# Splitting the first state load in two, and moving or putting off VectorE work that stood ahead of batch 1's A^T

## The chip, the cores and the metric

One NeuronCore of a Trainium2 chip runs the whole program. The metric is the device time of one execution in microseconds (us), the median over several executions. A profile is one execution: its "span" leaves out some 2 us of start and end that the time includes. Ratios are the mean time of one kernel's fast executions over that of the other's of the same rounds, so not quite the ratio of the medians quoted.

## The reference, cut to what matters

```python
B, H, S, Ns, D = 8, 8, 512, 32, 64
scores = x @ state.T / sqrt(D);  a  = softmax(scores)        # x reads the states
xread  = a @ state
scores2 = state @ x.T / sqrt(D); a2 = softmax(scores2)       # the states read x
sread  = a2 @ x
y = concat([xread, sread]) -> (4352, 512)
out = maximum(y @ w1, y @ w2) @ w_out                        # d_ff = 1024
```

The kernel folds the MoE weights into the states: `wcat` holds W1 - W2 (1024 columns) and W2 @ Wout (512 columns), and per batch `SW = states @ wcat`. Layer 1 of a batch is then `relu(SW^T A^T)`, and layer 2 (l2) adds `r @ Wout` to `A @ SW[:, 1024:]`. So each batch needs x transposed (`xt`) for its scores, the scaled exponents `a`, their transpose `aT`, and SW in three parts of 512 columns.

## The kernel before: the parts that matter

Loads, all on SyncE's (SP's) queue, in this order (s_f are states, xf is x, w2f/w1f/wof the weights):

```python
first, rest = slice(0, 3), slice(3, 8)
load_states(first)                 # 192 KB in rows of 256 B
load_x(0, 2)                       # two halves of 512 KB
for ch in range(2):
    load_w(w2f, moe_w2, ch); load_wo(2 * ch); load_wo(2 * ch + 1)
load_w(w1f, moe_w1, 0); load_w(w1f, moe_w1, 1)     # "W1b" in what follows: the first one, w1f -> w1b
load_x(1); load_states(slice(3, 8)); load_x(2)
```

Every engine runs its list in program order. The stretch that the change reorders (batch 0's second half beside batch 1's scores):

```python
compact_x(1, 0); compact_x(1, 1)   # ACT: two casts of x to bf16, 1.0 us each
d_xt(1)                            # transpose by DMA
...
u_sw(0, 1); l2_add(0, 3, ...); l1(0, {}, range(4, 8))
u_exp(1, 0); u_exp(1, 1)           # TensorE scores, ACT exp
u_norm(1, 0, nc.vector)            # DVE: sum, reciprocal, scaling a <- e, er
u_norm(1, 1, nc.gpsimd)            # the scaling on GpSimd
cast_x(2)
l2_add(0, 0, range(4, 8)); l2_close(0, 0)          # l2_close: copy PSUM -> SBUF, DVE for even, ACT for odd
u_sw(1, 0)                                         # SW part 0 of batch 1: matmuls, a copy on DVE, one on ACT
u_sr(1)
l2_add(0, 1, range(4, 8)); l2_close(0, 1)
u_sw(1, 1)
compact_x(2, 0); compact_x(2, 1); d_xt(2)          # ACT, then DMA
l2_add(0, 2, range(4, 8)); l2_close(0, 2)
u_sw(1, 2); u_at(1, "V")                           # A^T: TensorE transposes, copy on DVE
l2_add(0, 3, ...); u_srt(1); l2_close(0, 3); l2_out(0)
for b in range(1, B): l1(b, fill) ...              # regular from here
```

The softmax here doesn't subtract the row's maximum and nothing guards it: scores larger than these inputs give would overflow.

Of the kernel before, what the change touches and what calls it, by code (L numbers as in the profile page):

```python
# [15 lines left out]
def kernel(  # L16
# [14 lines left out]
    nc = tc.nc  # L31
# [5 lines left out]
    NC = S // 128  # L37
# [15 lines left out]
    def bank(dtype=F32, kind="ps"):  # L53
        return pools[kind].tile([128, 512 if dtype == F32 else 1024], dtype, tag="b", name=kind)
# [4 lines left out]
    def copy(eng, o, i):  # L59
        if eng == "A":  # L60
            nc.scalar.copy(o, i)  # L61
        elif eng == "V":
            nc.vector.tensor_copy(o, i)  # L63
        else:
            nc.gpsimd.tensor_copy(o, i)  # L65
# [4 lines left out]
    def run(*units):  # L70
        for u in units:
            u()
# [4 lines left out]
    def load_x(b, parts=1):  # L77
        xf_t[b] = xio.tile([128, H, NC * D], F32, tag="xf", name="xf")
        for g in range(parts):
            nc.sync.dma_start(out=xf_t[b][:, g::parts, :], in_=x[b, g::parts].rearrange("h (p c) d -> p h (c d)", c=NC))  # L80
# [3 lines left out]
    def load_states(bs):  # L84
        nc.sync.dma_start(out=s_f[:, 2 * bs.start:2 * bs.stop],
                          in_=state[bs].rearrange("b (q h) n d -> (h n) (b q) d", q=2))

    first, rest = slice(0, 3), slice(3, 8)
    w2f = stage.tile([128, 4, FF], F32)
    w1f = stage.tile([128, 4, FF], F32)  # L90
    wof = stage.tile([128, NF, DM], F32)
# [1 line left out]
    def load_w(t, w, ch):  # L93
        cs = slice(ch * 512, (ch + 1) * 512)
        nc.sync.dma_start(out=t[:, :, cs], in_=w.rearrange("(i p) f -> p i f", p=128)[:, :, cs])
# [10 lines left out]
        load_wo(2 * ch + 1)  # L106
    load_w(w1f, moe_w1, 0)
    load_w(w1f, moe_w1, 1)
    load_x(1)
    load_states(slice(3, 8))  # L110
    load_x(2)

    ident = consts.tile([128, 128], BF16)
# [20 lines left out]
    def cast_states(eng, bs):  # L134
        qs = slice(2 * bs.start, 2 * bs.stop)
        copy(eng, s_bf[:, qs], s_f[:, qs].unsqueeze(2).to_broadcast([128, qs.stop - qs.start, 2, D]))
# [12 lines left out]
    def states(bs):  # L149
        p = bank(BF16)  # L150
        n = bs.stop - bs.start
        for q in range(2 * n):
            nc.tensor.transpose(p[:, q * 128:(q + 1) * 128], s_bf[:, 2 * bs.start + q].rearrange("p u d -> p (u d)"), ident)
        for g in range(2):
            copy("V", sbd[64 * g:64 * g + 64, bs, :, g, :],
                 p[64 * g:64 * g + 64, 0:256 * n].rearrange("p (b h n) -> p b h n", b=n, h=H))
# [16 lines left out]
    def cast_x(b, parts=(("P", slice(0, 8)),)):  # L173
        new_x(b)
        xp = st[b]["xp"] = xio.tile([128, H, NC, 66], BF16, tag="xp", name="xp")
        nc.gpsimd.memset(xp[:, :, :, 64:65], 1.0)
        for e, hs in parts:
            copy(e, xp[:, hs, :, 0:64], xf_t[b][:, hs].rearrange("p h (c d) -> p h c d", c=NC))

    def compact_x(b, g, eng="A"):  # L180
        new_x(b)
        if g == 0:
            st[b]["xc"] = at.tile([128, H, NC * D], BF16, tag="xc", bufs=1, name="xc")
        copy(eng, st[b]["xc"][:, 4 * g:4 * g + 4], xf_t[b][:, 4 * g:4 * g + 4])


    def d_xt(b):
        nc.sync.dma_start_transpose(out=st[b]["xt"], in_=st[b]["xc"].rearrange("p h w -> p (h w)"))
# [14 lines left out]
    def u_exp(b, g):  # L203
        d = st[b]
        if g == 0:
            d["e"] = at.tile([128, 2, 4, NC, Ns], BF16, tag="e", name="e")
            d["es"] = at.tile([128, 2, 4 * NC], F32, tag="es", name="es")
            d["er"] = at.tile([128, 2, 4 * NC], F32, tag="er", name="er")
            d["a"] = at.tile([128, 2, NC, 4, Ns], BF16, tag="a", name="a")
        p = bank()  # L210
        for i in range(4):
            for cp in range(2):
                k = 2 * i + cp
                nc.tensor.matmul(p[:, k * 64:k * 64 + 64],  # L214
                                 d["xt"][:, 4 * i + 2 * g + cp, :], sbd[:, b, 2 * i + g].rearrange("p u n -> p (u n)"),
                                 start=(k == 0), stop=(k == 7))
        nc.scalar.activation(out=d["e"][:, g].rearrange("p i c n -> p (i c n)"), in_=p, func=ACTF.Exp, scale=scale)  # L217

    def u_norm(b, g, mul):
        d = st[b]  # L220
        nc.vector.tensor_reduce(d["es"][:, g], d["e"][:, g].rearrange("p i c n -> p (i c) n"),  # L221
                                axis=mybir.AxisListType.X, op=ALU.add)
        nc.vector.reciprocal(d["er"][:, g], d["es"][:, g])
        mul.tensor_mul(  # L224
            d["a"][:, g].rearrange("p c i n -> p i c n"), d["e"][:, g],
            d["er"][:, g].rearrange("p (i c) -> p i c", i=4).unsqueeze(3).to_broadcast([128, 4, NC, Ns]))
# [41 lines left out]
    def sw_mm(b, ch, engs="VA"):  # L268

        pg = [bank(kind="acc" if ch == 2 and b > 1 else "ps") for g in range(2)]  # L270

        two = (b, ch) == (0, 0)
        terms = ((sbd, w1b), (sneg, w2b)) if two else ((sbd, wcat),)
        for k, (sv, w) in enumerate(terms):
            for i in range(4):
                for g in range(2):
                    gs = slice(64 * g, 64 * g + 64)
                    nc.tensor.matmul(pg[g][32 * i:32 * i + 32, :],  # L278
                                     sneg[gs, i, :] if k else sbd[gs, b, 2 * i + g, g, :],
                                     w[gs, i, ch * 512:(ch + 1) * 512],  # L280
                                     start=(k == 0), stop=(k == len(terms) - 1))
        return lambda: [copy(engs[g], SW[b][:, g, ch * 512:(ch + 1) * 512], pg[g]) for g in range(2)]

    def u_sw(b, *chs):
        for out_of in [sw_mm(b, ch) for ch in chs]:
            out_of()
# [4 lines left out]
    def relu(o, p, eng=None):  # L291
        flip[0] ^= 1
        if eng == "A" or (eng is None and flip[0]):
            nc.scalar.activation(out=o, in_=p, func=ACTF.Relu)  # L294
        else:
            nc.vector.tensor_scalar(o, p, scalar1=0.0, scalar2=None, op0=ALU.max)  # L296
# [3 lines left out]
    def l1(b, fill, fs=range(NF), engs=None):  # L300
        if fs[0] == 0:
            R[b] = big.tile([128, NF, NC * 128], BF16, tag="r", name="r")
        for f in fs:
            p = bank()
            for g in range(2):
                nc.tensor.matmul(p, SW[b][:, g, f * 128:(f + 1) * 128], AT[b][:, g, :], start=(g == 0), stop=(g == 1))  # L306
            relu(R[b][:, f, :], p, engs and engs[f - fs[0]])
            run(*fill.get(f, ()))
# [3 lines left out]
    def l2_open(b, c):  # L312
        if c == 0:
            OB[b] = [big.tile([128, NC, DM], F32, tag="ob", name="ob")] + [None] * NC
        OB[b][1 + c] = acc()
        for g in range(2):
            nc.tensor.matmul(OB[b][1 + c], AT[b][:, g, c * 128:(c + 1) * 128], SW[b][:, g, FF:WC], start=(g == 0), stop=False)  # L317

    def l2_add(b, c, fs):
        for f in fs:  # L320
            nc.tensor.matmul(OB[b][1 + c], R[b][:, f, c * 128:(c + 1) * 128], wo[:, f, :], start=False, stop=(f == NF - 1))  # L321

    def l2_close(b, c):
        ob = OB[b][0]
        dst = out[b * L:b * L + S].rearrange("(p c) n -> p c n", c=NC)
        copy("A" if c % 2 else "V", ob[:, c, :], OB[b][1 + c])
        if b == B - 1:
            nc.sync.dma_start(out=dst[:, c:c + 1], in_=ob[:, c:c + 1])

    def l2_out(b):  # L330
        nc.sync.dma_start(out=out[b * L:b * L + S].rearrange("(p c) n -> p c n", c=NC), in_=OB[b][0])
# [156 lines left out]
    compact_x(1, 0)  # L488
    compact_x(1, 1)
    d_xt(1)  # L490
    cast_states("P", rest)
    cast_x(1)
    load_x(3)
    sT = d_states(rest)
    for c in range(NC):
        l2_open(0, c)
    for c in range(NC - 1):
        l2_add(0, c, range(0, 4))
    u_sw(0, 1)
    l2_add(0, 3, range(0, 4))  # L500
    l1(0, {}, range(4, 8))
    u_exp(1, 0)
    u_exp(1, 1)
    u_norm(1, 0, nc.vector)
    u_norm(1, 1, nc.gpsimd)
    cast_x(2)
    l2_add(0, 0, range(4, 8))
    l2_close(0, 0)
    u_sw(1, 0)
    u_sr(1)  # L510
    l2_add(0, 1, range(4, 8))
    l2_close(0, 1)
    u_sw(1, 1)
    compact_x(2, 0)
    compact_x(2, 1)
    d_xt(2)
    l2_add(0, 2, range(4, 8))
    l2_close(0, 2)
    u_sw(1, 2)
    u_at(1, "V")  # L520
    l2_add(0, 3, range(4, 6))
    u_srt(1)
    l2_add(0, 3, range(6, 8))
    l2_close(0, 3)
    l2_out(0)
    for b in range(1, B):
        fill = fillers(b)
# [40 lines left out]
```

## Time and profile before

| | us |
|---|---|
| time, median of 6 executions | 151.78 (151.63 to 151.95) |
| span of the profiled execution | 149.5 (that execution: 151.25, faster than any unprofiled one) |
| TensorE busy | 139.9, 94% of the span |
| VectorE (DVE), ScalarE (ACT), GpSimd (POOL) busy | 82.3, 75.0, 42.8 |

The prediction shows the lines of the chain of waits and of TensorE's waits. To read the chain: each line is the piece of work that the end waited for at that time, so an engine named there is what the kernel stood on; what is not named there can be busy without costing anything.

### The profile page before, as it was taken

What the parts mean: (1) busy time and instruction counts of PE and PEld (TensorE: products, weight loads), DVE (VectorE), ACT (ScalarE), POOL (GpSimd) and SP (SyncE); (2) the same over time, 40 slices, a digit from 0 to 9 for tenths busy, and PEclk for the clock granted to TensorE, in tenths of its full rate; (3) what the DMA queues carried; (4) which work ended last, traced back from release to release, by engine and by line L of the source; (5) the groups of instructions that cost most, each with busy time, mean ns of one, the idle gap of its engine ahead of it and who ended that gap; (6) DMA issues with size and microseconds to landing.
All of it is one profiled execution on the core that took longest, in us unless ns stands there. A gap on an engine that the chain in (4) does not pass through costs nothing.

```text
span 149.5 us, 2991 instructions
## 1 busy us (share of the span) xinstructions
PE 139.9 (94%) x1229; PEld 67.7 (45%) x1249; DVE 82.3 (55%) x149; ACT 75.0 (50%) x126; POOL 42.8 (29%) x45
## 2 busy tenths in 40 slices
PE   6988999999799999999999999999999999999990
PEld 1454633424345445434543454344445434764460
DVE  5538528947968097726754582658067625721120
ACT  3157447545958157626844682478167036521010
POOL 3145359670934510550073017104100500000000
PEclk9999999999999999999999999999999999999999
DMA  4999999988599958983979397850556031502423
GB/s 112 381 387 387 388 385 326 293 157 262 113 246 295 266 110 259 305 154 87 289 253 203 117 304 206 154 246 35 111 104 281 2 75 44 237 0 70 142 96 120
DMA packets 37950, 29.89 MB, mean 200 GB/s; under 512 B 24880, under 2 KB 33328, under 8 KB 37040
## 3 DMA queue, kind: packets, MB, share of 16 engines
q1 hardware_dynamic: 37792, 29.56, 68.0%
q8 instruction: 10, 0.16, 0.4%
q10 hardware_dynamic: 144, 0.13, 0.3%
q14 instruction: 4, 0.03, 0.1%
HBM read 15.20 MB, written 8.91 MB: 161 GB/s over the span
## 4 chain that ended last, share of the span: by engine, by line
PE 73%; DMA 13%; DVE 6%; SPq 4%; issue 2%; ACT 1%
PE acc L321 32%; PE ps L306 18%; DMA w1f<-in_moe_w_dram 10%; PE acc L317 9%; DMA xt<-xc 3%; PE ps L365 2%; PE acc L375 2%; PE ps L278 2%; PE ps L214 2%; SPq L98 2%; DVE swt L63 2%; PE acc L355 1%; PE ps L237 1%; PE acc L373 1%; DVE es L221 1%
## 5 line engine op out<-in xcount | busy, mean ns | idle before, releaser
L321 PE MATMUL acc<-wo,r 128*128 128x512 bf16 x239 | 58.3, 379 | 0.6 <-issue 0.2
L321 PEld LDWEIGHTS <-r 128*128 128x128 bf16 x248 | 23.9, 98 | 28.5 <-issue 0.5
L296 DVE TENSOR_SCALAR r<-ps 128x512 bf16<-128x512 f32 x32 | 22.1, 691 | 14.7 <-PE ps L306 14.7
L306 PE MATMUL ps<-aT,swt 128*128 128x512 bf16 x127 | 29.1, 379 | 1.2 <-DVE aT L63 0.9
L224 POOL TENSOR_TENSOR a<-e,er 128x512 bf16<-128x512 bf16 x13 | 13.4, 1049 | 57.3 <-ACT e L217 27.2
L63 DVE COPY ob<-acc 128x512 f32<-128x512 f32 (+1 forms) x17 | 11.1, 652 | 30.2 <-PE acc L321 29.8
L61 ACT COPY ob<-acc 128x512 f32<-128x512 f32 (+1 forms) x16 | 9.1, 572 | 28.6 <-PE acc L321 21.0
L294 ACT ACTIVATE r<-ps 128x512 bf16<-128x512 f32 x32 | 19.2, 601 | 7.0 <-PE ps L306 6.4
L306 PEld LDWEIGHTS <-swt 128*128 128x128 bf16 x128 | 12.1, 98 | 15.8 <-issue 1.1
L317 PE MATMUL acc<-swt,aT 128*128 128x512 bf16 x56 | 16.7, 380 | 1.0 <-issue 1.0
L61 ACT CAST swt<-ps 128x512 bf16<-128x512 f32 x18 | 9.9, 588 | 14.0 <-PE ps L278 14.0
L65 POOL CAST xp<-xf 128x2048 bf16<-128x2048 f32 (+1 forms) x8 | 14.1, 1761 | 9.1 <-DMA xf<-in_x_dram 9.1
L61 ACT CAST xc<-xf 128x1024 bf16<-128x1024 f32 x14 | 14.0, 1052 | 1.1 <-DMA xf<-in_x_dram 1.1
L221 DVE TENSOR_REDUCE es<-e 128x16 f32<-128x512 bf16 x16 | 10.6, 662 | 4.0 <-ACT e L217 4.0
L63 DVE CAST swt<-ps 128x512 bf16<-128x512 f32 x18 | 11.7, 680 | 1.2 <-PE ps L278 1.2
L217 ACT ACTIVATE e<-ps 128x512 bf16<-128x512 f32 x16 | 8.8, 595 | 1.3 <-PE ps L214 0.6
L129 PE MATMUL ps<-warm 128*128 128x512 bf16 x24 | 8.2, 470 | 1.3 <-POOL warm L115 1.3
L410 PE MATMUL acc<-wo,w2t 128*128 128x512 bf16 x30 | 7.3, 379 | 0.1
L317 PEld LDWEIGHTS <-aT 128*128 128x128 bf16 x62 | 4.7, 98 | 6.0 <-issue 2.6
L278 PE MATMUL ps<-wcat,sbd 64*32 64x512 bf16 x136 | 6.3, 382 | 0.4 <-DVE swt L63 0.4
L214 PEld LDWEIGHTS <-xt 128*128 128x128 bf16 x128 | 4.7, 98 | 3.2 <-DMA xt<-xc 0.8
L214 PE MATMUL ps<-sbd,xt 128*128 128x64 bf16 x128 | 5.2, 193 | 0.9 <-ACT xt L61 0.6
(73 smaller groups left out, 114.8 us busy)
## 6 DMA issues: line engine op xcount, KB each, us to landing
xf<-in_x_dram SPq DMA_DIRECT2D x7, 1024.0 KB, 7.5
out_dram<-ob SPq DMA_DIRECT2D x7, 1024.0 KB, 5.0
w2f<-in_moe_w_dram SPq DMA_DIRECT2D x2, 1024.0 KB, 9.2
wof<-in_moe_w_out_dram SPq DMA_DIRECT2D x4, 512.0 KB, 10.4
w1f<-in_moe_w_dram SPq DMA_DIRECT2D x2, 1024.0 KB, 15.1
xf<-in_x_dram SPq DMA_DIRECT2D x2, 512.0 KB, 4.7
out_dram<-ob SPq DMA_DIRECT2D x3, 256.0 KB, 2.4
out_dram<-obs SPq DMA_DIRECT2D x8, 64.0 KB, 1.7
```

Source lines behind the costliest of these rows:

```text
L61: nc.scalar.copy(o, i)
L63: nc.vector.tensor_copy(o, i)
L65: nc.gpsimd.tensor_copy(o, i)
L214: nc.tensor.matmul(p[:, k * 64:k * 64 + 64], d["xt"][:, 4 * i + 2 * g + cp, :], sbd[:, b, 2 * i + g].rearrange("p u n -> p (u n)"), start= ...
L221: nc.vector.tensor_reduce(d["es"][:, g], d["e"][:, g].rearrange("p i c n -> p (i c) n"), axis=mybir.AxisListType.X, op=ALU.add)
L224: mul.tensor_mul(d["a"][:, g].rearrange("p c i n -> p i c n"), d["e"][:, g], d["er"][:, g].rearrange("p (i c) -> p i c", i=4).unsqueeze(3) ...
L278: nc.tensor.matmul(pg[g][32 * i:32 * i + 32, :], sneg[gs, i, :] if k else sbd[gs, b, 2 * i + g, g, :], w[gs, i, ch * 512:(ch + 1) * 512], ...
L294: nc.scalar.activation(out=o, in_=p, func=ACTF.Relu)
L296: nc.vector.tensor_scalar(o, p, scalar1=0.0, scalar2=None, op0=ALU.max)
L306: nc.tensor.matmul(p, SW[b][:, g, f * 128:(f + 1) * 128], AT[b][:, g, :], start=(g == 0), stop=(g == 1))
L317: nc.tensor.matmul(OB[b][1 + c], AT[b][:, g, c * 128:(c + 1) * 128], SW[b][:, g, FF:WC], start=(g == 0), stop=False)
L321: nc.tensor.matmul(OB[b][1 + c], R[b][:, f, c * 128:(c + 1) * 128], wo[:, f, :], start=False, stop=(f == NF - 1))
```

## The change

Its intent: get x and the weights sooner by letting only batch 0's states lead the queue, and shorten the DVE's run in front of batch 1's A^T.

```diff
-    first, rest = slice(0, 3), slice(3, 8)
+    first, second, rest = slice(0, 1), slice(1, 3), slice(3, 8)
     ...
     load_w(w1f, moe_w1, 1)
+    load_states(second)
     load_x(1)
-    load_states(slice(3, 8))
+    load_states(rest)
     ...
+    cast_states("P", second)
     cast_states("P", rest)
     ...                               # states(second): transposes behind l2_add(0, 1)
     l1(0, {}, range(4, 8))
+    u_sw(1, 0)
     u_exp(1, 0)
     u_exp(1, 1)
-    u_norm(1, 0, nc.vector)
+    u_norm(1, 0, nc.gpsimd)
     ...
-    l2_close(0, 0)
-    u_sw(1, 0)
+    u_sw(1, 1)
     u_sr(1)
     ...
     l2_close(0, 1)
-    u_sw(1, 1)
     compact_x(2, 0)
     ...
-    l2_close(0, 2)
     u_sw(1, 2)
     u_at(1, "V")
     ...
-    l2_close(0, 3)
+    for c in (3, 0, 2):
+        l2_close(0, c)
```

More of the change, by code (lines that the diff above doesn't have):

```diff
@@ L496 @@
         l2_open(0, c)
-    for c in range(NC - 1):
-        l2_add(0, c, range(0, 4))
+    l2_add(0, 0, range(0, 4))
+    l2_add(0, 1, range(0, 4))
+    states(second)
+    l2_add(0, 2, range(0, 4))
     u_sw(0, 1)
```

## The prediction

> **What bounds the kernel now.** I read the page first (one core, clock 0.999, so no throttle to argue about), then the chain that ended last in order of time, the waits of the TensorE, and the timeline of the first 45 us. From about 45 us to the end the chain is TensorE alone, batch after batch. So the question is what makes it reach that regular part at 45.00 us and not sooner. The chain of waits up to there, cut:
>
> ```profile
> 6.44 15.09 DMA w1f<-in_moe_w_dram
> 21.55 0.69 DVE w1b L63
> ...
> 24.14 1.90 PE ps L306 x8
> ...
> 29.36 4.35 DMA xt<-xc
> 33.75 0.42 PE ps L214 x8
> 34.20 0.61 ACT e L217
> 34.83 0.70 DVE es L221
> ...
> 37.41 0.55 DVE ob L63
> 37.95 0.59 DVE swt L63
> ...
> 39.54 0.60 DVE ob L63
> 40.14 0.60 DVE swt L63
> 40.74 0.61 DVE aT L63
> 41.39 2.96 PE ps L306 x13
> 44.35 0.05 issue
> 44.41 0.59 PE ps L306 x2
> 45.00 0.47 PE ps L214 x16
> ```
>
> Columns are start, length, what. The reader is to see three pieces: the load stream up to 21.55 (weights W1), a transpose by DMA of x of batch 1 from 29.36 to 33.7, and then a run of VectorE (DVE) work from 34.83 to 41.35 without a hole, which ends in the copy of A^T of batch 1. Everything after it is TensorE. The waits of the TensorE say how much idle time that is:
>
> ```profile
> PE ps L306 <- DVE aT L63: 0.9, 1, 0.9
> PE ps L214 <- DMA xt<-xc: 0.3, 1, 0.3
> PE ps L278 <- DVE swt L63: 0.4, 1, 0.4
> PE ps L278 <- DVE w1b L63: 0.2, 1, 0.2
> ```
>
> Only 1.8 us of idle TensorE in all (0.9 + 0.3 + 0.4 + 0.2) lies in this stretch. The work in the TensorE's list does not shrink, so about 1.6 us (without the 0.2) is what the later half of the change can win at most; what wins it first is the 0.9.
>
> **What the Trainium skill says.** "TensorE: Matmul & The Clock Gate", the table of specifications, gives ScalarE, VectorE and GpSimd a strict first-in first-out queue. The trace agrees: the A^T copy stands behind two l2 copies and three SW copies in the DVE's list and starts only at 40.74, though its transposes were through at 39.61 (they start at 39.00 and last 0.61). "GPSIMD Engine Reference", section Engine selection, calls two-input elementwise work on GpSimd about twice as slow as on VectorE. Here the scaling a<-e,er took 0.69 us on DVE and 1.05 on GpSimd, a ratio of 1.5: less bad than the page. "DMA: Bandwidth & Descriptors", Specifications, puts full transfer rate at 512 B and more; a state row is 64 floats, 256 B. The trace agrees: in quarter-microsecond windows the first state load ran at 209 to 279 GB/s, the x and W loads after it at 385 to 393.
>
> **Part 1, the load queue.** The first state load goes from 192 KB to 64 KB. Between 1.75 and 3.25 us the queue moved 66, 209, 279, 254, 176 and 94 GB/s in six quarters, which is 269 kB; 197 of it were states, so 73 kB of x. With a third of the states, x is held only by its own issue: states had data moving about 1.0 us after their issue at 0.74, x is issued at 1.25, so x flows from 2.3 or 2.4. From there to 3.25 at a rising rate of around 300 GB/s gives 260 kB instead of 73, and 190 kB at 387 GB/s is 0.45 to 0.5 us. Everything up to W1 comes 0.45 us earlier, so W1's first half lands at 21.1, and the chain through DVE w1b, wcat, swt to the first layer-1 matmul (24.14) starts at 23.7. TensorE would follow by 0.3 to 0.45: its warm-up matmuls get ahead by only four 128-column transposes.
>
> But the 128 KB come back ahead of x of batch 1. The later load of 320 KB of states pulled the stream from 350 GB/s to 300, 259, 237 and 264 over four halves of a microsecond: 530 kB where 700 would have gone, a loss of 0.49 us, and 328 kB at 350 is another 0.94. So 320 KB cost 1.43 us and 128 KB cost 0.57. x of batch 1 lands at 27.34 - 0.45 + 0.57 = 27.46, 0.1 later than now. ScalarE (ACT) was idle 1.1 us waiting for it, so its two compaction casts (2.0 us) and the transpose (landing 4.3 us after issue) follow: x^T of batch 1 at 33.85. **The head start of W1 therefore does not get through**; it ends in front of this transpose.
>
> **Part 2, TensorE up to batch 1's scores.** It now ends its list at 33.42 and waits 0.3. After: 33.42 - 0.4 + four state transposes (0.25; six took 0.6 with the clock still low) + SW part 0 of batch 1 moved up (0.43) = 33.7. That fits the hole and ends at the new landing. The state casts lie in a GpSimd hole: it waits 1.4 us for the late states and the new cast of 512 elements costs 1.92 x 512/1280 = 0.77. The two copies into the block-diagonal tile (64x768 took 0.555, so 64x512 about 0.4 each) stand on DVE between its subtractions, which end at 29.6 now (29.2 after), and the SW copy at 30.4. No new wait.
>
> **Part 3, the DVE run.** Scores at 33.9 instead of 33.75, exponent at 34.35, first sum at 35.0 instead of 34.83. Of the 6.5 us run these go: one scaling 0.69, two l2 copies 2 x 0.6, SW part 0's copy 0.6 (moved ahead, at 34.0 to 34.7, beside the exponent). That is 2.5 off 41.35, plus 0.15, 39.0. But other things are now close behind. GpSimd: reciprocal at 35.95, two scalings of 1.05, so a is done at 38.05. TensorE: scores 33.9 to 34.4, l2 0.87, SW 0.45, state read 0.4, l2 0.87 twice, SW 0.43, giving 38.3 for the A^T transposes, which last 0.6; then l2 and the small transpose till about 39.8. The A^T copy ends at 39.6. So layer 1 of batch 1 starts at about 39.8, by TensorE alone, instead of 41.39: 1.6 us earlier, the whole idle sum.
>
> **Part 4, what catches it.** Layer 1 lasts 3.6 us, then the scores of batch 2 need x^T of batch 2. These lines of the timeline and of the tile xt give it (before):
>
> ```profile
> 37.93 2.00 ACT L61 CAST xc<-xf 128x1024 bf16<-128x1024 f32 x2
> 39.96 2.63 SPq L188 DMA_TRANSPOSE xt<-xc  x1
> DMA to landing us min/median/max: 4.2/4.3/4.3
> ```
>
> It lands at 44.2 now, 0.8 ahead of its use at 45.00. ACT's list keeps the l2 copy of quarter 1 ahead of the compaction, and that copy still comes at 37.0 to 37.1, since as many matmuls stand before it as now. Only the SW copy between the two moves forward. So compaction starts at about 37.65 instead of 37.93, and the transpose lands at 43.95. TensorE would be there at 43.4 to 43.6 (ACT evacuates SW part 2 only after the compaction, and the late l2 copies delay the first relus by a few tenths). **It waits some 0.4 us for this transpose**, and the scores of batch 2 run at 43.95 instead of 45.00. After that everything is relative to TensorE, so this 1.05 us goes to the end: 151.76 - 1.05 = **150.7 us**.
>
> **Rivals.** (a) The full idle sum gets through, because compaction starts sooner than I think: 1.6 us, 150.2. For it: I place the ACT by small differences. Against it: the l2 copy ahead of compaction waits for the TensorE's same matmuls. (b) 128 KB of short rows cost more in the middle than I work out (landings follow the slowest of 16 DMA engines); x of batch 1 lands 0.5 us later, all behind it moves with it, and 0.4 us remain: 151.3. For it: the short state loads are the slow part of the stream; against it: the whole queue carries the same bytes and rows up to there. (c) GpSimd becomes the bound: its scalings end 0.25 us before the A^T transposes want them. If the state cast of 1.92 us lands later and its x cast runs over, or DVE slows it, 0.3 to 0.5 us go, but part of it is hidden in the wait for x^T of batch 2: 150.9. (d) The three late l2 copies hold PSUM banks and the DVE and ACT in layer 1 of batch 1: worth 0.2 to 0.4, also hidden by that wait.
>
> **Range and chances.** The sum of idle time caps the gain near 1.6 plus at most the 0.45 of part 1 if x of batch 1 comes early too; nothing in the change adds work to TensorE (four transposes move, none is new). So 150.0 to 151.5, centre 150.7. Over 2% would need 3 us, twice what the stretch has of idle: 0.02. Slower by 2%: 0.01.
>
> **What would show it.** W1's first half lands near 21.1; x of batch 1 near 27.5, its transpose near 33.85; A^T's copy before 39.7 and layer 1 of batch 1 near 39.8; then a new wait of scores on xt<-xc of some 0.4 us before about 44.0. From the scores of batch 2 to the end the time is as now (149.5 - 45.0 = 104.5). It is wrong if x of batch 1 lands over 0.4 us off, if the A^T transposes wait for GpSimd, or if the part after 45 us gets longer.

## The result, and the profile after

151.42 us (151.08 to 151.81, 6 executions) against 151.78: ratio 0.9977, 95% interval 0.9960 to 0.9993. A gain of 0.36 us by the medians, where 1.05 was predicted. In a second call the changed kernel took 151.39 against 151.67 (ratio 0.9989, 0.9977 to 1.0001). So the change is worth 0.2 to 0.4 us, a third of the forecast or less, at 151.4 just inside the range.

The chain of waits of the changed kernel (start, length, what), the part that answers to the one shown of before. Lines of the changed file stand one or three lower (L307 for L306, L215 for L214):

```profile
6.24 15.41 DMA w1f<-in_moe_w_dram
21.65 0.02 issue
21.68 0.69 DVE w1b L63
...
24.27 1.90 PE ps L307 x8
...
30.07 4.78 DMA xt<-xc
34.85 0.05 issue
34.90 0.66 PE ps L215 x16
...
38.60 1.99 ACT xc L61 x2
40.59 0.03 ACT swt L61
40.62 4.30 DMA xt<-xc
44.92 0.04 issue
44.96 0.64 PE ps L215 x16
```

The DVE run that ended in the A^T copy is gone from the chain, as intended. In its place stand two DMA transposes, of x of batch 1 (to 34.85) and of batch 2 (to 44.92), with ACT's compaction between. (In a second trace of the changed kernel the first of them is nearly a tie: x^T of batch 1 landed at 34.6, and the chain goes through ACT's copy of SW part 0, now ahead of the scores, which ended at 34.70.) TensorE's waits say the same (engine, what it waited for, us in total, times, longest):

```profile
PE ps L215 <- DMA xt<-xc: 1.5, 2, 0.8
PE ps L307 <- DVE swt L63: 0.3, 1, 0.3
```

The wait for the A^T copy (0.9) has disappeared and the one for `xt` has grown from 0.3 to 1.5. The spans of both profiles are 149.5, so these two traces alone show no gain at all; the trace of before was a lucky execution (151.25). A second trace of the kernel before (151.79) is used beside the first.

The starts in the timelines (us; where a kernel has two traces, both):

| kernel | x of batch 0, half 1 used | W1b used | x of batch 1 used | scores of batch 1 | layer 1 of batch 1 | scores of batch 2 |
|---|---|---|---|---|---|---|
| before | 5.48 / 5.37 | 21.55 / 21.65 | 27.34 / 27.43 | 33.75 / 34.30 | 41.39 / 41.93 | 44.84 / 45.38 |
| changed | 5.32 / 5.21 | 21.68 / 21.59 | 28.05 / 27.99 | 34.90 / 34.69 | 40.69 / 40.48 | 44.96 / 45.08 |
| predicted | about 5.0 | 21.1 | 27.46 | 33.9 | 39.8 | 43.95 |

The prediction counts the scores of batch 2 from 45.00, not 44.84: that is the start of their piece in the chain, which begins where the piece before it ends; the table has the start of their first instruction.

W1b is not earlier, and x of batch 1 is 0.6 to 0.7 later. Why W1b's head start failed shows at the very start of the stream, in quarter-microsecond windows (columns: window, then busy us and instruction counts of TensorE, its weight loads, DVE, ACT and GpSimd, the granted clock, the mean share of the DMA engines, GB/s). Before:

```profile
2.25:2.50 0.25, 0.25 (x2) 0.04 (x1) 0.25 (x1) 0.00 (x0) 0.00 (x0) 1.00 1.21 279
2.75:3.00 0.25, 0.25 (x3) 0.00 (x1) 0.25 (x1) 0.00 (x0) 0.00 (x0) 1.00 1.32 176
3.00:3.25 0.25, 0.25 (x2) 0.15 (x1) 0.00 (x0) 0.00 (x0) 0.00 (x0) 1.00 0.37 94
3.25:3.50 0.25, 0.25 (x2) 0.00 (x0) 0.16 (x1) 0.00 (x0) 0.00 (x0) 1.00 0.82 254
```

And changed:

```profile
2.25:2.50 0.25, 0.25 (x2) 0.04 (x1) 0.25 (x1) 0.00 (x0) 0.00 (x0) 1.00 0.43 110
2.75:3.00 0.25, 0.25 (x3) 0.00 (x1) 0.25 (x2) 0.00 (x0) 0.00 (x0) 1.00 0.10 29
3.00:3.25 0.25, 0.25 (x2) 0.15 (x1) 0.14 (x1) 0.00 (x0) 0.00 (x0) 1.00 0.13 33
3.25:3.50 0.25, 0.25 (x2) 0.08 (x1) 0.00 (x0) 0.00 (x0) 0.00 (x0) 1.00 0.65 225
```

The short state load is through by about 2.5 us, and then the queue stands nearly still (29 and 33 GB/s; 57 and 106 in a second trace) until 3.25, where x begins to flow in earnest, just where it began before. The states of batches 1 and 2 had lain in time in which x did not flow anyway: taking them away freed a stretch that nothing could use. The single packets that the traces list say the same: the first half megabyte of x had moved by 4.58 and 4.68 us in the two traces of before, by 4.66 and 4.61 in the two of the changed kernel.

### The profile page after: what moved, and what is told of

It reads as the page before. It is cut to its first block, busy times and chain, and to the rows that moved or that the text cites. A ratio compares the mean times of both kernels' runs of the same rounds, so it can differ in the third digit from the quotient of the medians.

```text
span 149.5 us, 2995 instructions
## 1 busy us (share of the span) xinstructions
PE 140.1 (94%) x1228; PEld 67.7 (45%) x1249; DVE 81.7 (55%) x150; ACT 74.9 (50%) x126; POOL 45.3 (30%) x47
## 4 chain that ended last, share of the span: by engine, by line
PE 73%; DMA 16%; SPq 3%; DVE 2%; issue 2%; ACT 2%
PE acc L322 33%; PE ps L307 15%; DMA w1f<-in_moe_w_dram 10%; PE acc L318 9%; DMA xt<-xc 6%; PE ps L279 2%; PE ps L215 2%; PE ps L366 2%; PE acc L376 2%; SPq L98 2%; PE ps L238 2%; PE acc L356 1%; ACT xc L61 1%; PE acc L374 1%; PE acc L279 1%
## 5 line engine op out<-in xcount | busy, mean ns | idle before, releaser
L225 POOL TENSOR_TENSOR a<-e,er 128x512 bf16<-128x512 bf16 x14 | 14.4, 1050 | 54.8 <-ACT e L218 39.1
L307 PE MATMUL ps<-aT,swt 128*128 128x512 bf16 x127 | 29.1, 379 | 0.3 <-DVE swt L63 0.3
L63 DVE COPY ob<-acc 128x512 f32<-128x512 f32 (+1 forms) x17 | 11.1, 655 | 30.2 <-PE acc L322 29.8
L307 PEld LDWEIGHTS <-swt 128*128 128x128 bf16 x128 | 12.1, 98 | 14.9 <-DVE swt L63 0.9
L63 DVE CAST swt<-ps 128x512 bf16<-128x512 f32 x18 | 11.6, 679 | 0.9 <-PE ps L279 0.9
L130 PE MATMUL ps<-warm 128*128 128x512 bf16 x24 | 8.7, 493 | 1.3 <-POOL warm L116 1.3
L215 PE MATMUL ps<-sbd,xt 128*128 128x64 bf16 x128 | 5.2, 193 | 2.0 <-DMA xt<-xc 1.5
L215 PEld LDWEIGHTS <-xt 128*128 128x128 bf16 x128 | 4.6, 98 | 4.4 <-DMA xt<-xc 2.3
```

The lines of the kernel that those rows point to most:

```text
L63: nc.vector.tensor_copy(o, i)
L215: nc.tensor.matmul(p[:, k * 64:k * 64 + 64], d["xt"][:, 4 * i + 2 * g + cp, :], sbd[:, b, 2 * i + g].rearrange("p u n -> p (u n)"), start= ...
L225: mul.tensor_mul(d["a"][:, g].rearrange("p c i n -> p i c n"), d["e"][:, g], d["er"][:, g].rearrange("p (i c) -> p i c", i=4).unsqueeze(3) ...
L307: nc.tensor.matmul(p, SW[b][:, g, f * 128:(f + 1) * 128], AT[b][:, g, :], start=(g == 0), stop=(g == 1))
```

## The experiments

The theory after this result, **A**: the 128 KB of state rows moved ahead of x of batch 1 cost their 0.6 us there, unpaid, because the head start never came; the new order on TensorE and DVE wins what was forecast, and the two nearly cancel. Its rivals: **B**, the traces are two unlucky and lucky draws; **C**, the new order wins nothing because the put-off copies come back as a backlog; **F**, splitting the load hurts wherever it stands; **D**, something other than batch 2's transpose caps what is left. On the head start alone there is **G**: x begins to flow about 2 us after its own issue, whatever stands in front of it.

All kernels gave the right result. Times are medians of five or six executions, or four where said; before was 151.67 to 151.82.

### The changed kernel and the kernel before, once more

No edit.

> The changed kernel once more, unedited, to see how far its load stream varies. Theory A (the 128 KB of state rows now ahead of x of batch 1 cost more than the 0.45 us the head was to win) expects x of batch 1 to land near 28.05 us again (27.34 before), x^T of batch 1 at 34.9 and the scores of batch 2 at 45.0. Rival B (the first trace was an unlucky run; the stream usually does win) expects 27.4 to 27.6 and 44.0 to 44.4. Time 151.2 to 151.6 either way.

> The kernel before once more, for a second trace of it: its first profiled execution took 151.25 us, below every unprofiled one (151.44 to 151.95), so its landing times may be on the early side. Theory A wants W1b's first half at 21.5 to 21.8, x of batch 1 at 27.3 to 27.6 and the scores of batch 2 at 45.0 to 45.4. If x of batch 1 lands as late as in the changed kernel (28.0), the cost of the moved state rows is not shown by the traces.

Measured: the changed kernel 151.39; the table above has the starts. x of batch 1 at 27.99 (28.05 in the first trace) against 27.43 (27.34): rival B falls, the delay is in every trace. What B had right is the transpose behind it, which landed 4.35 us after its issue in the first trace of before and 4.8 in the second, so that the first comparison made the scores of batch 1 look 1.15 later; against the second trace it is 0.6 and 0.4.

### Each half alone

Order alone: the old loads, with the changed order.

```diff
 # against the changed kernel
-first, second, rest = slice(0, 1), slice(1, 3), slice(3, 8)
+first, rest = slice(0, 3), slice(3, 8)
-load_states(second); cast_states("P", second); states(second)
```

> The loads as before (states of batches 0 to 2 first), only the order of batch 0's l2 copies, SW part 0 of batch 1 and the scalings as in the changed kernel. Theory A: x of batch 1 lands at 27.3 as before, its scores run at 33.8, the compaction of x of batch 2 starts 0.3 sooner than before and the scores of batch 2 run at 43.9 to 44.0 after a wait of 0.4 on that transpose; 150.7 us. Rival C (putting the copies off wins nothing whatever the loads, because a backlog on DVE and ACT gives it back): 151.4 to 151.8, with layer 1 of batch 1 longer than 3.7 us.

Loads alone: the new loads and the new place of `states(second)`, with the old order of everything else.

> The new loads alone (batch 0's states first, batches 1 and 2 behind W1b, their transposes where the changed kernel has them), the rest in the order of before. Theory A: x of batch 1 near 28.0, x^T 0.7 to 1.1 us later than before, everything behind it moved, 152.4 to 152.9 us: slower than before by 0.5 to 0.7 per cent. Rival B: 151.3 to 151.8, no worse than before.

Measured: the order alone took 150.88 us (ratio 0.9944, 0.9930 to 0.9958), the loads alone 152.32 (1.0046, 1.0034 to 1.0058). So the order wins 0.8 and the loads lose 0.65; together they nearly cancel, as theory A says and C denies. In the loads-alone trace x of batch 1 is used from 28.05 and layer 1 of batch 1 starts at 42.60, with the old wait for the A^T copy (0.9) behind it. The starts of the order-alone trace were 0.3 to 0.8 later than I expected (scores of batch 1 at 34.39, of batch 2 at 44.73), as its head was slow in that execution (151.24 us, the slowest of the six): first layer-1 matmul at 24.84 instead of 24.1 to 24.3. The gain stands on the timed executions.

### Where the second state load stands

```diff
-load_states(second)
 load_x(1)
+load_states(second)
 load_states(rest)
```

> The changed kernel with the second state load issued behind x of batch 1 instead of ahead of it. Theory A (what hurts is the 128 KB ahead of x of batch 1): x of batch 1 lands at 27.1 to 27.4, its scores run 0.5 to 1 us sooner than in the changed kernel, 150.7 to 151.0 us, as with the old loads and the new order. Rival F (what hurts is splitting the states into one load more, or transposing batches 1 and 2 inside the l2 of batch 0, wherever the load stands): no better than the changed kernel, 151.3 to 151.6.

Measured: **150.76 us** (0.9936, 0.9919 to 0.9954), 0.6 better than the changed kernel by one moved line. The use of x of batch 1 in the timeline (start, us, engine, line, what, [idle before, released by]), of this kernel:

```profile
27.30 1.99 ACT L61 CAST xc<-xf 128x1024 bf16<-128x1024 f32 x2 [1.11 <-DMA xf<-in_x_dram]
...
34.06 0.70 PE L215 MATMUL ps<-sbd,xt 128*128 128x64 bf16 x16
...
44.42 0.64 PE L215 MATMUL ps<-sbd,xt 128*128 128x64 bf16 x16 [0.89 <-DMA xt<-xc]
```

and of the changed kernel:

```profile
28.05 1.99 ACT L61 CAST xc<-xf 128x1024 bf16<-128x1024 f32 x2 [1.68 <-DMA xf<-in_x_dram]
...
34.90 0.64 PE L215 MATMUL ps<-sbd,xt 128*128 128x64 bf16 x16 [0.80 <-DMA xt<-xc]
...
44.96 0.64 PE L215 MATMUL ps<-sbd,xt 128*128 128x64 bf16 x16 [0.66 <-DMA xt<-xc]
```

The reader is to see the bracket of the first lines: ACT waits 1.68 us for x with the states in front, 1.11 with them behind. Rival F falls: the load split as it is costs nothing there. This kernel runs nearly on the prediction's timetable (34.06 for 33.9, layer 1 of batch 1 at 39.91 for 39.8), and TensorE then waits 0.89 for batch 2's transpose, the wait forecast at 0.4.

### The start of the stream

x of batch 0 issued ahead of its states:

```diff
-load_states(first)
 load_x(0, 2)
+load_states(first)
```

> The changed kernel with x of batch 0 issued ahead of the states of batch 0. It tells what sets when x starts to flow. Theory G (x starts about 2 us after its own issue, whatever stands in front of it in the queue; the head start of the shorter state load was hidden in that): x's halves land about 0.5 us sooner than in the changed kernel (5.32 and 6.80), because it is issued 0.5 us sooner. If the 64 KB of states still held it (my prediction's view), 0.2 us. In time at most 0.3 us better than the changed kernel, as x of batch 1 stays late.

Measured: 155.90 us, a miss in time. x could be used at 4.64, 0.6 to 0.7 sooner than in the changed kernel's two traces. The windows (columns as above) show when it began to flow:

```profile
2.50:2.75 0.25, 0.25 (x2) 0.15 (x1) 0.25 (x1) 0.00 (x0) 0.00 (x0) 1.00 0.08 25
2.75:3.00 0.25, 0.25 (x3) 0.01 (x1) 0.24 (x1) 0.00 (x0) 0.00 (x0) 1.00 1.01 356
```

x was issued at 0.74 and flowed in earnest from 2.75, with nothing in front of it: 2.0 us, as with 64 KB or 192 KB of states in front (issued at 1.25, from 3.25). That is theory G, and it is why the shorter state load gave no head start. But the 64 KB of states, now queued behind 1 MB of x, were usable only at 6.45 instead of 2.91. TensorE waited 3.0 us for them, and DVE's list, in order, stood too. The 4.5 us lost against the changed kernel (151.4) hide everything else. One thing was not expected: GpSimd's share of W1b could be used at 20.15, against 21.5 to 21.8 in every other kernel.

Then the states of batch 0 on ACT's queue, x first on SP's, in the kernel with the second load behind:

```diff
-load_states(first)
+nc.scalar.dma_start(...)     # the same load, issued by ACT
```

> The second state load behind x of batch 1, and batch 0's states issued from ACT's queue, so that x of batch 0 is first on SP's queue and issued 0.5 us sooner, without states queued behind it as in x_first. Theory G: x's halves land 0.4 to 0.6 us sooner than with the load moved alone (5.12 and 6.63). Whether that reaches the first layer-1 matmul (24.09) tells if the start of the stream sets W1b's landing: if so 23.6 and 150.2 to 150.5 us; if something later in the stream does (W1b landed at 21.5 to 21.8 in all kernels whatever x did), no change, 150.6 to 150.9.

Measured: two groups, 150.72 and 150.90 in two executions, 152.17 to 152.49 in four, all at a full clock; the profile is of the fastest. In it x landed at 5.01 (the seven other traces with the second load behind x of batch 1 have 5.12 to 5.59) and W1b at 21.52, as everywhere. The timing is inconclusive. What it adds: the 0.1 to 0.6 us that x wins here at the start of the stream are not seen at W1b. W1b does not follow x: leaving out the kernel with x first, x varies from 5.01 to 6.24 in the traces, and W1b stays within 21.49 to 21.81 (21.52 with the earliest x, 21.69 with the latest). The packets tell part of why. W1b is the fifth of six megabytes of weights. The first five megabytes' worth of weight packets had moved by 19.62 and 19.72 us in the two traces of before, 19.68 in both of the changed kernel, and 19.42 here; when W1b could be used, 5.6 to 5.8 of the six had moved (5.3 in the kernel with x first). So W1b waits for a last part that lags some 2 us behind the stream as a whole, and the few tenths that the stream won here did not show. What makes that part late is not known.

### What caps the new order

Compaction of batch 2's x right behind batch 1's exponents (old loads):

```diff
 l2_add(0, 0, range(4, 8))
+compact_x(2, 0); compact_x(2, 1); d_xt(2)
 u_sw(1, 1)
 ...
-compact_x(2, 0); compact_x(2, 1); d_xt(2)
```

> As order_only, and the compaction of x of batch 2 on ACT put right behind the exponents of batch 1, ahead of SW part 1 and l2 copy 1, so that its transpose cannot be what the scores of batch 2 wait for. If that transpose is what caps order_only (theory A): the scores of batch 2 run at 43.4 to 43.6, TensorE idle only in front of layer 1 of batch 1, 150.2 to 150.4 us. If it does not cap (rival D: DVE or GpSimd does), the same as order_only within 0.1.

The transpose of the late states (`sT`) behind that of x of batch 2 (old loads):

```diff
-sT = d_states(rest)
 ...
 d_xt(2)
+sT = d_states(rest)
```

> Old loads, new order, and the transpose by DMA of the states of batches 3 to 7 issued behind that of x of batch 2 instead of ahead of it. It tells whether the wait of the scores of batch 2 comes from ACT's late compaction (then no change, 150.8 to 151.0 us, since the state transpose was through by 40.5) or from transposes queued ahead in the DMA rings (then the transpose lands up to 0.5 us after issue sooner, 150.4 to 150.7).

Measured: 151.06 and 150.99 against 150.88 for the order alone: neither helps. The first is instructive. ACT did compact from 35.76 instead of 38.35 and the transpose was issued at 37.77 instead of 40.37, but it took 6.7 us to land instead of 4.4. So the scores of batch 2 ran at 44.48, still behind a wait of 0.71 for `xt`: what was won at the issue was lost on the way. One suspect is the transpose of the states, which goes ahead of it on the same queue; the other edit takes it from there. Both edits together, on the kernel with the second load behind x of batch 1:

> The second state load behind x of batch 1, and both remedies for the wait of 0.9 us that is left: compaction of x of batch 2 right behind the exponents of batch 1, and the transpose of the late states behind it. With the compaction moved alone its transpose took 6.7 us instead of 4.5[...]. Theory A: now it lands at 41 to 42, TensorE waits for nothing before the scores of batch 2, which run at 43.5: 150.0 to 150.3 us. Rival D (another wait takes its place: the SW copies that ACT now does later, or a loss further on): 150.6 to 150.9, no better than with the load moved alone.

Measured: **150.22 us** (four executions, 150.16 to 150.27; ratio 0.9899, 0.9884 to 0.9913). Of its timeline:

```profile
35.66 1.99 ACT L61 CAST xc<-xf 128x1024 bf16<-128x1024 f32 x2
...
43.80 0.64 PE L215 MATMUL ps<-sbd,xt 128*128 128x64 bf16 x16
```

The scores of batch 2 have no bracket any more: the wait of 0.89 in front of them is gone. But this is nearly a tie, not a transpose out of the way. The chain of this trace still goes through it:

```profile
37.67 6.08 DMA xt<-xc
43.75 0.05 issue
43.80 0.64 PE ps L215 x16
```

It landed at 43.75, and layer 1 ended at about 43.67. So batch 2's transpose was the cap, as the prediction had it and against rival D, and of the edits tried it took both to bring it down to TensorE's own time. This version beats both kernels, by 1.5 us and 1.2 us. The same two edits on the old loads:

> The old loads (states of batches 0 to 2 first) with the new order, compaction early and state transpose late. It tells what the shorter first load is worth when the second stands behind x of batch 1: if W1b and x of batch 1 land at the same time with either load order (21.6 and 27.4), then the same as 150.22 within 0.2. If the shorter first load wins 0.3 or more at the head: 150.5 to 150.7.

Measured: 150.29 us (0.9903, 0.9882 to 0.9924), the same within the scatter. So the shorter first load is worth nothing measurable, even with its second part out of the way. (The chain of this trace is TensorE alone there, with the scores of batch 2 at 43.81.)

How much of the slow transpose was the other transpose is another matter. From issue to landing, batch 2's x took:

| issued at | states' transpose | us to landing |
|---|---|---|
| 39.73 to 40.37 | ahead (order alone) or behind (states' transpose late) | 4.3 and 4.4 |
| 39.8 to 41.2, ten more traces | ahead | 4.2 to 5.0 |
| 37.77 | ahead (compaction early) | 6.7 |
| 37.67 to 37.78 | behind (both edits, on new and old loads) | 6.0 to 6.1 |
| same two edits, with copies or scaling back (below) | behind | 6.4 and 6.5 |

So the transpose in front explains at most some 0.6 us of the 2.3, and with the late issue it made no difference. The landing at 43.75 instead of 44.5 was just enough. Where the extra time goes can be seen, why cannot: in each of the five traces with the early issue the queue all but stops for a whole microsecond on the way (6 and 10 GB/s from 40.5 to 41.5 in the 150.22 us kernel, 11 and 9 from 41.0 to 42.0 with the compaction alone moved), and in the traces of the first row it does not (no half microsecond under 172 GB/s from 41.5 to 43.5). The load of batch 3's x, which flowed until about 38, was over by then.

### What the new order wins

On the kernel with the second load behind x of batch 1, three of the order's parts were undone one at a time:

```diff
 # copies back                 # scaling back                    # SW part 0 back
 l2_add(0, 0, range(4, 8))     -u_norm(1, 0, nc.gpsimd)          -u_sw(1, 0)
+l2_close(0, 0)                +u_norm(1, 0, nc.vector)           u_exp(1, 0)
 ...                                                              ...
 l2_add(0, 2, range(4, 8))                                        l2_add(0, 0, range(4, 8))
+l2_close(0, 2)                                                  +u_sw(1, 0)
 ...                                                              u_sw(1, 1)
```

> The second state load behind x of batch 1, and l2 copies 0 and 2 of batch 0 back at their old places. The DVE run gets 1.26 us longer, so layer 1 of batch 1 starts near 41.0 instead of 39.9; the wait of 0.9 for the transpose of batch 2 hides most of that: 150.9 to 151.3 us if my sum holds (0.2 to 0.5 slower than with them put off); 151.7 if the copies were all of the gain.

> The second state load behind x of batch 1, and the first scaling of batch 1 back on DVE. The DVE is then 0.69 longer before the second sum, GpSimd has one scaling instead of two. The A^T transposes wait for the later of the two; whatever it is, below 0.9 it hides in the wait for the transpose of batch 2: no change, 150.6 to 150.9 us. If GpSimd's two scalings in a row were a bound that reaches the end, it would be faster by 0.2 or more.

> The second state load behind x of batch 1, with SW part 0 of batch 1 back behind the scores of batch 1 (in front of part 1). If moving it ahead of the scores is what the new order gains (0.43 of TensorE in front of a wait, and its copies off the ACT in front of the compaction): scores of batch 1 at 33.8, the l2 matmuls of quarter 1 and with them ACT's copy 1 and the compaction 0.4 to 0.6 later, scores of batch 2 at 44.8 to 45.0, 151.2 to 151.5 us. If it is not: 150.7 to 150.9.

And the first two again where nothing hides them, in the 150.22 us kernel:

> The kernel without the wait for the transpose of batch 2 (second state load behind x of batch 1, compaction early, state transpose late; 150.22), with l2 copies 0 and 2 back at their old places. If the late copies are worth their sum once nothing hides it: layer 1 of batch 1 starts 0.6 us later (0.58 was measured with the copies back: 40.49 against 39.91) and the time is 150.7 to 150.9. If they are worth nothing even so: 150.1 to 150.35.

> The same kernel with the first scaling of batch 1 back on DVE. GpSimd starts its only scaling after the second reciprocal on DVE, which comes 0.69 later, and ends near the same time as two in a row; the DVE's SW copy 1 comes later. If the scaling's place matters with nothing hiding it: 150.5 to 150.8; if not: 150.1 to 150.4.

| undone | in the 150.76 kernel (ratio 0.9936) | in the 150.22 kernel (ratio 0.9899) |
|---|---|---|
| l2 copies 0 and 2 put off | 150.84 (0.9942) | 150.52 (0.9909) |
| first scaling on GpSimd | 150.86 (0.9936) | 150.46 (0.9912) |
| SW part 0 ahead of the scores | 151.46 (0.9974) | not run |

Putting the copies off and moving the scaling, two of the three things that shorten the DVE run, are worth nothing in time while TensorE waits for batch 2's transpose: with the copies back, layer 1 of batch 1 started at 40.49 instead of 39.91 and the scores of batch 2 at 44.37 instead of 44.42. Without that wait each may be worth 0.2 to 0.3 by the medians, of calls apart, and the intervals of the ratios overlap (0.9893 to 0.9924 and 0.9896 to 0.9929 against 0.9884 to 0.9913), so that is not clear of the noise. Nor is it clear of the transpose: the chains of these two traces do run through the DVE work that was put back (layer 1 at 40.59 and 40.28 instead of 40.04), but batch 2's x^T also landed 0.4 later in them (44.1 instead of 43.75), so the loss cannot be given to the one or the other. Moving SW part 0 in front of the scores is what counts: 0.7 us by the medians, with intervals that do not touch (0.9960 to 0.9988 against 0.9919 to 0.9954). Its trace has the compaction of batch 2's x at 38.78 instead of 37.82, and the scores of batch 2 at 45.17 instead of 44.42: one SW part less stands between the scores and ACT's l2 copy 1, behind which the compaction waits. With it back, the chain there holds its matmuls (0.42) and ACT's copy of it (0.59), for which TensorE waits.

## Why the prediction was wrong, point by point

- **"Everything up to W1 comes 0.45 us earlier" failed; this is the step that broke the sum.** I counted x as flowing at around 300 GB/s from 2.3 or 2.4 us once the states were out of its way. Its first packet did move at 2.4, but the queue then ran at 29 to 66 GB/s from 2.50 to 3.25; x flowed in earnest from 3.25 with either load, 2.0 us after its own issue. x of batch 0 could be used 0.16 sooner in both pairs of traces, and W1b no sooner (21.55 and 21.65 before, 21.68 and 21.59 after). The term should have been 0. The warning sign was there: before, too, the queue fell to 94 GB/s at 3.00 to 3.25, between the states and x, which is idle time that states could not have caused.
- **"128 KB cost 0.57" held.** x of batch 1 was used from 28.05, 27.99 and 28.05 in the three traces with the states ahead of it, from 27.34 to 27.63 in the six traces with the old loads: 0.56 between the means, 28.03 and 27.47. But I had set it against the 0.45 that did not exist, and so took 0.1 for the net where 0.6 was due. Adding those 0.45 us to the predicted 150.7 gives 151.15, most of the way to 151.4. That states are slow at 209 to 279 GB/s was read off the queue's first microsecond, where x alone, in the kernel with x first, ran slower still (8 and 25 GB/s from 2.25 to 2.75); the later load, at 237 to 300, is the sounder sign.
- **"The scores of batch 2 run at 43.95 instead of 45.00" compared two things.** 45.00 is the start of a piece of the chain, 43.95 that of an instruction; the instruction of before started at 44.84. By it the forecast gain is 0.9 and not 1.05. With both terms mended the forecast is 1.05 less 0.45 less 0.15, some 0.45 us; 0.36 was measured.
- The sum of TensorE's idle time left out a line of the same view, `PE ps L306 <- DVE swt L63: 0.3`: it is 2.1 us, not 1.8. Nothing rested on it but the limit of the range.
- **"The head start of W1 does not get through; it ends in front of this transpose"**: right that x^T of batch 1 sets the scores, but I used this to say that the size of the head start did not matter, when the landing of x of batch 1 had it as a term.
- **The state casts and transposes are not a new wait**: held in TensorE's waits, though GpSimd's cast of 512 elements took 1.61 us where I scaled 0.77.
- **The DVE run shortened, layer 1 of batch 1 by TensorE alone**: held in mechanism. The changed kernel's wait for A^T is gone; from scores to layer 1 it took 5.8 us in both traces (34.90 to 40.69, 34.69 to 40.48) against 5.9 predicted and 7.6 before. What I misjudged is the worth of the parts: the copies and the scaling, most of what I summed, do not reach the end; SW part 0 does, and by ACT's list more than by DVE's.
- **"It waits some 0.4 us for this transpose"**: the wait came as forecast, at about double the size: 0.66 and 0.98 in the two traces of the changed kernel, 0.89 with the second load moved.
- **"From the scores of batch 2 to the end 104.5"**: held to 0.1, 149.5 - 44.96 = 104.5 (from 44.84 it was 104.7 before).
- Of the rivals, (b) came true in its number (151.3) and in x of batch 1 landing some 0.5 later, but not in its reason: the short rows did not cost more than worked out, the credit against them was missing. That its 151.3 is near the measured time is luck. (a) would have needed compaction sooner, which one of the experiments then made.

Open: what makes the last part of W1b lag until 21.5 to 21.8 whatever x does, when it landed at 20.1 in the kernel whose TensorE was 4 us late; what stops the queue for a microsecond in the transposes issued at 37.7 us, which take 6.0 to 6.7 us where those issued at 40 to 41 take 4.2 to 5.0; and what makes the slow group with two issuing queues.

## What to carry to other kernels

A transfer at the head of a queue costs those behind it only as much as they could have flowed in its place: look for a gap between the two in fine windows before crediting its removal. What is taken from the head has to stand somewhere else, and in a full stream it is paid there in full, so put it behind the transfer that the next wait is for. And when a run of one engine is shortened, find the next arrival that its end meets, here a transpose that hung on another engine's list, and that took longer when it was issued sooner; until that moves, most of the shortening is worth nothing.

## What the Trainium skill lacked or had wrong

- "DMA: Bandwidth & Descriptors", Latency and other measured facts, gives about 0.6 us to the first byte of a load issued by SyncE. Here the first packet of x moved 1.1 us after the start of its issue (1.25 to 2.4), some 0.6 after the end of that 0.5 us instruction, so this fits; but x flowed in earnest only at 3.25, with or without 128 KB more states in front, and the page has no figure for the time to full flow (2.0 us here).
- The same page gives the transpose by DMA a bandwidth (261 GB/s, more where contiguous) and no latency. Here 512 KB landed 4.2 to 5.0 us after issue, and 6.0 to 6.7 us when issued at 37.7, for a reason that the runs did not settle. 512 KB over 4.3 us is 122 GB/s; while it flowed, the queue ran at 211 to 221 GB/s (before, 41.5 to 43.5).
- "GPSIMD Engine Reference", Engine selection: two-input work about twice as slow as on VectorE, one-input at about line rate. The scaling (two inputs) was 1.5 times as slow, 1.05 against 0.69 us. A one-input cast of 512 columns took 1.61 us beside DVE's long subtractions, and one of 1280 columns 1.76 us in the same trace; the page's words on the shared port name such contention, without a number for it.
